# New written-out engine orders and 66 instead of 70 warming products in a fused linear-attention and MLP kernel

## The chip, the cores and the metric

The kernel runs on one NeuronCore of a Trainium2 chip. The engines named here are PE (TensorE, matrix products; PEld are its weight loads), DVE (VectorE), ACT (ScalarE), POOL (GpSimd) and SP (SyncE, which here issues every DMA). Each runs its own instructions strictly in their order; they wait for one another by semaphores. Results of products go to PSUM, which the kernel uses as eight banks of 128 partitions by 512 f32 values.

The metric is the device time of one execution in microseconds, as the median of several runs. The span of a profile goes from the first to the last instruction of one profiled execution.

## The reference

The input x is 2048 tokens by 512, in bf16. Two residual layers follow one another:

```python
# layer A: linear attention, 32 heads of 16
qkv = layernorm(x) @ wqkv                       # 512 x 1536
phi = lambda t: where(t > 0, t + 1, exp(t)) + 1e-6
pq, pk = phi(q), phi(k)
kv  = einsum("bhsd,bhse->bhde", pk, v)
z   = einsum("bhsd->bhd", pk)
o   = einsum("bhqd,bhde->bhqe", pq, kv) / (einsum("bhqd,bhd->bhq", pq, z)[..., None] + 1e-6)
h   = x + o @ wo                                # 512 x 512
# layer B: MLP with relu
out = h + relu(layernorm(h) @ w1) @ w2          # 512 x 1792, 1792 x 512
```

## The kernel before, in words

The 2048 tokens are 16 tiles of 128, in four chunks of four tiles. No scheduler sets the order. One long text, ORDER, is a list of words; the kernel goes through it from left to right and calls for each word the function `op_` of its name with the numbers behind it. So the text fixes, engine by engine, the order of the instructions. Two words on different engines have no order but what data and buffers ask for; two words on one engine run as they stand. A word can issue several instructions: `K.3.7` means the four products of the K projection of tile 3 into bank 7.

The words that matter, with their engine, and t for a tile, c for a chunk:

- Loads on SP: `lx.t.n` (n tiles of x), `lk`, `lq`, `lv`, `lo`, `l1`, `l2` (the parts k to k+n of wk, wq, wv, wo, w1, w2). SP's DMAs share eight completion semaphores in turn, so each also waits for the one eight before it.
- Warming on PE: `warm.n.b.w`, n products of zeros, w columns wide (L245).
- Layer norm of x: `S`, `A` (statistics, DVE, L248, L249), `R` (1/sqrt by a logarithm and an exponential, ACT, L254, L255), `N` (normalise, DVE, L262). Transposing a tile for the products: `T` on PE and `E` on ACT (tiles 0 to 4), or `X`, a DMA transpose issued by SP (L308, tiles 5 to 15).
- Projections on PE: `K.t` (L316, reads tile t's transposed norm as weights), `Q.c.j` (L324, reads all four tiles of a chunk).
- phi: `F` and `U` (exponential and relu out of the bank, ACT, L334, L337), `M` and `D` (DVE, L341, L344); with a `q` in front for the queries.
- State: `G.t` (PE, L368) sums the outer products over all tiles in banks 4 to 7; `gA`, `gD` take them out; `za`, `zf`, `zhi`, `zlo`, `z`, `zc`, `zh` make the sum z; `kv` (wv enters here), `kx`, `m` (wo enters here), `mA`, `mD` make the matrix that each query is multiplied with.
- Denominators: `d4` (PE), `dl4`, `dx4` (reciprocal by logarithm and exponential, ACT), `wb` (written to DRAM), `rb` (eight loads that spread each of the rows of one chunk over 16 partitions, all into one tile `rr`), `dm` (DVE: queries times reciprocal, into `pqs`, L484).
- End of layer A: `h.t` (PE, L493), `hD` (plus x, DVE, L499). Layer norm of h: `s`, `a`, `r`, `n` or `nA`; transposes by PE (`t`, `v`) for tiles 2 and 3, by SP (`x`) for the others.
- MLP: `p.c.f` (PE, L508; `ph` is half a chunk wide, L517), `pD`, `pA` (relu out of two banks, L528, L523), `f.t.b.f0.n` (PE, L537: n of the 14 products of tile t, from the f0-th on), `fo` (scaled and added to h, DVE, L545), `fd` (stored, SP, L552). Tile 15 is done in three pieces of columns.

A bank must be read by ACT or DVE before PE may write it again. The words say which bank each product uses, so the choice of banks also sets which reader PE may have to wait for. The output tiles share four buffers, tile t using t mod 4.

Of the kernel before, what the change touches and what calls it, by code (L numbers as in the profile page):

```python
# [15 lines left out]


ORDER = """
table const masks warm.70.7.64 warm.2.7 lx.0.1 S.0 A.0 R.0.1 lx.1.1 S.1 lx.2.1 A.1 N.0 T.0.1 lk.0.4 S.2 R.1.1
N.1 T.1.2 lx.3.1 A.2 E.0 K.0.4 R.2.1 lx.4.2 S.3 N.2 T.2.1 E.1 A.3 S.5 R.3.1 K.1.0.0.2 K.1.0.2.2 N.3 S.4 A.5 A.4  # L20
E.2 T.3.2 K.2.6.0.2 K.2.6.2.2 F.0.1 M.0.1 lx.6.2 E.3 S.7 lq.0.4 R.4.2 lx.8.4 Q.0.3.1 N.4 U.0.1 A.7 F.1.1 F.2.1
T.4.2 N.5 S.6 Q.0.1.4 U.1.1 M.1.1 A.6 lx.12.4 M.2.1 D.0.1 R.6.2 K.3.7.0.2 K.3.7.2.2 E.4 X.5 U.2.1 U.3.1 D.1.1
N.6 Q.0.0.3 N.7 S.10 qF.0.0.2 K.4.5 K.5.6 S.8 A.10 S.9 A.8 qU.0.0.2 S.12 F.4.2 D.2.1 X.6 Q.0.2.0 A.9 A.12 K.6.2
S.13 S.11 M.4.2 A.11 A.13 U.4.2 D.4.2 F.3.1 R.8.2 N.9 M.3.1 X.7 K.7.3 R.12.2 R.10.2 N.8 F.6.2 D.3.1 N.13 S.15
G.0 G.1 U.6.2 S.14 X.9 X.8 N.10 A.14 A.15 N.12 qM.0.0.2 M.6.2 X.13 qF.0.2.2 R.14.2 qU.0.2.2 qM.0.2.2 N.11 G.2
G.3 G.5 G.4 N.14 X.12 K.9.3 K.8.2 K.13.1 N.15 qD.0.0.2 D.6.2 za.4.1 X.11 X.10 F.8.2 U.8.2 M.8.2 K.12.0 U.12.2
F.12.2 G.7 za.6.0 K.11.3 D.8.2 qD.0.2.2 M.12.2 za.8.0 K.10.2 F.10.2 X.14 G.8 K.14.0 U.10.2 X.15 K.15.1 M.10.2 zf
lv.2.2 lv.0.2 G.9 D.10.2 zhi D.12.2 F.14.2 G.6 G.10 G.11 M.14.2 zlo U.14.2 D.14.2 z.0.0 z.2.0 z.3.0 z.1.0 G.14
lo.0.2 lo.2.2 zc zh d4.0.1 dl4.0 l1.0.2 G.13 G.12 G.15 dx4.0 gA.2.2 Q.1.1.3 Q.1.0.2 qF.1.0.2 gD.0.2 kv.1.4
kv.3.4 kv.0.4 kv.2.4 kx qU.1.0.2 qM.1.0.2 qD.1.0.2 Q.1.3.1 Q.1.2.0 qF.1.2.2 m.0.2 m.1.3 mD.0.2 m.3.7 m.2.6 wb.0  # L30
Q.2.0.4 Q.2.1.5 rb.0.7 rb.0.1 rb.0.6 rb.0.3 rb.0.0 rb.0.2 rb.0.4 rb.0.5 l1.2.2 qM.1.2.2 qU.1.2.2 Q.2.3.1
qD.1.2.2 mA.2.2 qF.2.0.2 Q.2.2.0 qU.2.0.2 dm.0.2.2 dm.0.0.2 qM.2.0.2 h.1.6 hD.1 s.1 a.1 qU.2.2.2 d4.1.3 dl4.1
h.0.7 hD.0 s.0 dx4.1 h.2.6 h.3.5 a.0 l2.0.7 wb.1 hD.2 nA.1 hD.3 qF.2.2.2 nA.0 s.2 s.3 Q.3.0.2 Q.3.1.3 a.2
Q.3.3.6 a.3 qF.3.0.2 qU.3.0.2 Q.3.2.5 x.1 r.0.4 qF.3.2.2 n.2 t.2.7 n.3 t.3.4 qD.2.0.2 v.2 v.3 x.0 ph.0.3.1.0
ph.0.1.3.0 ph.0.2.0.0 ph.0.3.1.1 qM.2.2.2 qM.3.0.2 ph.0.0.2.0 ph.0.0.2.1 qM.3.2.2 qD.3.0.2 qU.3.2.2 qD.2.2.2
ph.0.2.0.1 qD.3.2.2 p.0.7.5 d4.2.6.2 pD.0.2.2 dl4.2 dl4.3 rb.1.4 rb.1.6 rb.1.3 rb.1.2 rb.1.0 rb.1.1 ph.0.1.3.1
rb.1.7 rb.1.5 p.0.6.4 dx4.2 dm.1.0.2 dm.1.2.2 h.4.0 pD.0.0.2 hD.4 pD.0.6.2 p.0.5.1 h.6.6 dx4.3 p.0.4.0 hD.6
l2.7.7 h.5.4 pA.0.4.2 s.4 s.6 hD.5 h.7.7 a.4 a.6 p.0.11.6 p.0.10.5 s.5 hD.7 a.5 p.0.9.4 wb.2 rb.2.6 n.4 rb.2.0
rb.2.4 s.7 n.6 rb.2.3 rb.2.2 rb.2.1 a.7 n.5 n.7 rb.2.5 rb.2.7 dm.2.0.2 dm.2.2.2 pD.0.10.2 p.0.13.1 p.0.12.0
p.0.8.3 pD.0.12.2 wb.3 r.4.4 rb.3.0 rb.3.4 h.10.7 hD.10 x.6 h.8.2 h.11.6 hD.8 s.10 rb.3.5 rb.3.1 rb.3.6  # L40
f.1.0.0.7 rb.3.3 rb.3.2 rb.3.7 s.8 hD.11 pD.0.8.2 h.9.5 f.3.1.0.7 x.7 x.5 s.11 a.8 hD.9 f.1.0.7.7 f.0.4.0.7 a.10
a.11 x.4 dm.3.2.2 dm.3.0.2 h.14.7 h.12.3 s.9 n.11 h.15.6 a.9 n.10 h.13.2 fo.1 n.9 n.8 hD.14 s.14 hD.12 x.11
hD.15 f.0.4.7.7 r.8.4 p.1.13.7 p.1.6.3 a.14 hD.13 s.12 s.15 s.13 a.12 a.15 a.13 n.14 p.1.12.6 n.13 f.3.1.7.7
n.12 n.15 p.1.2.5 fo.0 pD.1.12.2 x.10 p.1.7.4 fo.3 p.1.3.6 x.9 pD.1.6.2 pD.1.2.2 r.12.4 x.8 p.1.11.2 p.1.10.1
pD.1.10.2 f.2.4.0.7 p.2.0.6 p.2.1.7 f.2.4.7.7 pD.2.0.2 p.2.10.0 p.2.11.1 fo.2 x.14 p.2.6.2 p.2.7.3 x.15 fd.3
p.2.13.7 p.2.12.6 pD.2.10.2 pD.2.6.2 x.12 fd.1 pD.2.12.2 p.2.2.0 x.13 fd.0 p.2.3.1 p.1.5.6 p.1.4.5 pD.2.2.2
pD.1.4.2 p.1.0.3 p.1.1.4 p.1.9.1 p.1.8.0 pD.1.0.2 pD.1.8.2 f.4.4.0.7 f.4.4.7.7 fo.4 fd.4 f.5.3.0.7 f.5.3.7.7
fo.5 fd.2 f.6.7.0.7 f.6.7.7.7 fo.6 p.2.4.2 p.2.5.3 f.7.0.0.7 f.7.0.7.7 pD.2.4.2 fo.7 p.3.6.1 p.3.7.2 pD.3.6.2
p.3.8.3 p.3.9.4 p.3.5.1 pD.3.8.2 p.3.4.0 pD.3.4.2 fd.6 p.3.10.3 p.3.11.4 pD.3.10.2 p.3.2.0 p.3.3.1 p.3.0.5
p.3.1.6 pD.3.2.2 pD.3.0.2 p.3.13.3 fd.7 p.3.12.2 pD.3.12.2 f.10.1.0.7 f.15.2.0.14.3.1 f.15.7.0.14.0.2 p.2.8.4  # L50
p.2.9.5 fo.15.3.1 fd.15.3.1 fo.15.0.2 pD.2.8.2 f.8.7.0.7 f.10.1.7.7 fo.10 f.8.7.7.7 fo.8 f.14.2.0.7 f.14.2.7.7
f.13.3.0.7 fd.5 fd.8 fd.10 fo.14 f.13.3.7.7 fo.13 f.9.0.0.7 f.9.0.7.7 fd.15.0.2 f.11.6.0.7 f.11.6.7.7 fd.13 fo.9
f.12.0.0.7 fd.9 f.12.0.7.7 fo.11 fd.14 fd.11 fo.12 fd.12 f.15.2.0.14.2.1 fo.15.2.1 fd.15.2.1
"""


# [1 line left out]
def kernel(  # L58
# [253 lines left out]
    def op_K(t, b, k=0, n=KD):  # L312
        c, j = divmod(t, CT)
        at_bank["k", t] = b
        for kd in range(k, k + n):
            nc.tensor.matmul(  # L316
                bk[:, b, :], lhsT=lnT[c][:, kd, j * P : (j + 1) * P], rhs=wk_sb[:, kd, :],
                start=(kd == 0), stop=(kd == KD - 1),
            )
# [213 lines left out]
    def op_f(t, b, f0, n, k=0, w=KD):  # L533
        c, j = divmod(t, CT)
        at_bank["f", t, k] = b
        for f in range(f0, f0 + n):
            nc.tensor.matmul(  # L537
                bk[:, b, 0 : w * P], lhsT=acts[c % 2][:, f, j * P : (j + 1) * P],
                rhs=w2_sb[:, f, k * P : (k + w) * P],
                start=(f == 0), stop=(f == KF - 1),  # L540
            )
# [46 lines left out]
```

## Time and profile before

| | us |
|---|---|
| median of 3 runs | 169.87 |
| lowest and highest | 169.42 to 170.21 |
| profiled span, first to last instruction | 168.0 |
| median less span | 1.87 |
| PE busy | 162.7 |
| DVE busy | 115.6 |
| ACT busy | 49.5 |

The page shows one profiled execution; it gives its span, and what lies around the span is read here as the median less the span. In its rows a number before a comma is time, `x` counts instructions, and `<-` stands between what is written and what is read. In the rows of stretches of time each engine's busy time comes with the number of its instructions in brackets; then the granted PE clock, the busy share of the DMA engines and the GB/s. In the chain of waits the columns are start, length and what the time went to. In the timeline they are start, length, engine, line, operation, and in brackets the idle time before it and what ended it; neighbouring instructions of one kind are merged, with their count. Recorded lengths of neighbouring products overlap.

### The profile page before, as it was taken

The page shows a single profiled execution, that of the slowest core. Times are in us where ns is not written, and L with a number is a line of the kernel's source. Part 1 is how long each engine was busy: PE and PEld are TensorE (multiplying, and loading weights), DVE is VectorE, ACT ScalarE, POOL GpSimd, SP SyncE. Part 2 cuts the span into 40 slices and gives each one's busy share as a digit, 9 for nine tenths or more (in the row PEclk, how much of TensorE's full clock was granted, in tenths as well). Part 3 has the DMA queues.
Part 4 walks back from the last instruction along what each step waited for, and adds up shares of the span by engine and source line. Part 5 has one row for each costly group of instructions (what it writes and reads, how often), then busy time and mean ns, then how long its engine had stood idle before and what let it go on. Part 6 is the DMA issues. An engine that isn't in the chain of part 4 may idle for free.

```text
span 168.0 us, 2417 instructions
## 1 busy us (share of the span) xinstructions
PE 162.7 (97%) x924; PEld 79.2 (47%) x924; DVE 115.6 (69%) x217; ACT 49.5 (29%) x83; POOL 4.8 (3%) x21
## 2 busy tenths in 40 slices
...
GB/s 108 353 298 88 20 106 95 189 301 45 132 337 161 98 205 132 132 48 123 83 102 57 126 63 0 0 0 0 62 31 35 0 0 7 32 34 48 31 94 39
DMA packets 25003, 16.01 MB, mean 95 GB/s; under 512 B 15008, under 2 KB 23968, under 8 KB 24992
## 3 DMA queue, kind: packets, MB, share of 16 engines
...
q8 instruction: 7, 0.11, 0.3%
q14 instruction: 4, 0.03, 0.1%
...
## 4 chain that ended last, share of the span: by engine, by line
PE 92%; DMA 4%; SPq 2%; DVE 1%; issue 0%
PE bk L537 28%; PE bk L508 27%; PE bk L324 8%; PE bk L368 8%; PE bk L493 8%; PE bk L316 7%; DMA wq_sb<-in_A_wqkv_dram 4%; PE bk L517 2%; SPq L214 2%; PE bk L440 1%; DVE gT L545 1%; PE bk L392 1%; PE bk L414 1%; PE bk L426 1%; PE bk L287 0%
## 5 line engine op out<-in xcount | busy, mean ns | idle before, releaser
L537 PE MATMUL bk<-w_sb,at 128*128 128x512 bf16 (+2 forms) x252 | 50.0, 355 | 0.0
L508 PE MATMUL bk<-lnT,w_sb 128*128 128x512 bf16 x208 | 46.9, 379 | 0.0
L528 DVE TENSOR_SCALAR at<-bk 128x1024 bf16<-128x1024 f32 x27 | 32.8, 1223 | 13.2 <-PE bk L508 13.2
L537 PEld LDWEIGHTS <-at 128*128 128x128 bf16 x252 | 23.5, 98 | 25.4
L508 PEld LDWEIGHTS <-w_sb 128*128 128x128 bf16 x208 | 20.4, 98 | 23.9
L545 DVE SCALAR_TENSOR_TENSOR gT<-bk,rstd,h_nat 128x512 bf16<-128x512 f32 (+2 forms) x18 | 12.4, 691 | 24.6 <-PE bk L537 22.0
L334 ACT ACTIVATE eb<-bk 128x1024 bf16<-128x1024 f32 (+1 forms) x18 | 16.6, 929 | 5.3 <-PE bk L316 2.8
L337 ACT ACTIVATE rb<-bk 128x1024 bf16<-128x1024 f32 (+1 forms) x18 | 16.4, 929 | 0.0
L324 PE MATMUL bk<-lnT,wq_sb 128*128 128x512 bf16 x64 | 15.1, 379 | 0.3 <-DMA wq_sb<-in_A_wqkv_dram 0.3
L316 PE MATMUL bk<-wk_sb,lnT 128*128 128x512 bf16 x64 | 15.3, 379 | 0.0
L493 PE MATMUL bk<-m_sb,pqs 128*128 128x512 bf16 x64 | 15.1, 379 | 0.0
L368 PE MATMUL bk<-at,h_nat 128*128 128x512 bf16 x56 | 13.1, 379 | 0.0
L248 DVE BATCH_NORM_STATS2 st<-x_nat 128x6 f32<-128x512 bf16 x16 | 10.6, 678 | 2.3 <-DMA x_nat<-in_A_x_dram 2.3
L499 DVE TENSOR_TENSOR h_nat<-bk,x_nat 128x512 bf16<-128x512 f32 x16 | 10.6, 676 | 0.9 <-PE bk L493 0.9
L254 ACT ACTIVATE rstd<-mv,eps 128x2 f32<-128x2 f32 (+2 forms) x14 | 4.2, 297 | 23.7 <-DVE mv L251 20.9
L250 DVE BATCH_NORM_STATS2 st<-h_nat 128x6 f32<-128x512 bf16 x16 | 10.5, 684 | 0.1
L324 PEld LDWEIGHTS <-wq_sb 128*128 128x128 bf16 x64 | 6.1, 98 | 7.7 <-DMA wq_sb<-in_A_wqkv_dram 0.8
L493 PEld LDWEIGHTS <-pqs 128*128 128x128 bf16 x64 | 6.1, 98 | 7.7 <-DVE pqs L484 0.6
L368 PEld LDWEIGHTS <-h_nat 128*128 128x128 bf16 x64 | 6.1, 98 | 7.3 <-issue 0.2
L316 PEld LDWEIGHTS <-lnT 128*128 128x128 bf16 x64 | 6.1, 98 | 6.8
L341 DVE TENSOR_SCALAR eb<-eb 128x1024 bf16<-128x1024 bf16 (+1 forms) x18 | 6.6, 389 | 0.0
L262 DVE TENSOR_SCALAR h_nat<-x_nat,mv,rstd 128x512 bf16<-128x512 bf16 x16 | 6.3, 408 | 0.2 <-ACT rstd L255 0.2
...
## 6 DMA issues: line engine op xcount, KB each, us to landing
w_sb<-in_B_w_dram SPq DMA_DIRECT2D x4, 896.0 KB, 6.2
rr<-scr SPq DMA_DIRECT2D x32, 64.0 KB, 2.6
...
x_nat<-in_A_x_dram SPq DMA_DIRECT2D x2, 256.0 KB, 4.6
...
```

The costliest lines, as they stand in the source:

```text
L248: op_S = lambda t: nc.vector.bn_stats(out=st[:, t, :], in_=x_nat[:, t, :])
L316: nc.tensor.matmul(bk[:, b, :], lhsT=lnT[c][:, kd, j * P : (j + 1) * P], rhs=wk_sb[:, kd, :], start=(kd == 0), stop=(kd == KD - 1),)
L324: nc.tensor.matmul(bk[:, b, :], lhsT=wq_sb[:, kd, j * P : (j + 1) * P], rhs=lnT[c][:, kd, :], start=(kd == 0), stop=(kd == KD - 1),)
L334: nc.scalar.activation(out=buf(eb, kind, i, n), in_=bank(at_bank[kind, i], n), func=ACT.Exp)
L337: nc.scalar.activation(out=buf(rb, kind, i, n), in_=bank(at_bank[kind, i], n), func=ACT.Relu)
L368: nc.tensor.matmul(bk[:, KD + kd, :], lhsT=ln_nat[:, t, kd * P : (kd + 1) * P], rhs=pk(t)[:, 0, :], start=(not stated), stop=(len(stated) ...
L493: nc.tensor.matmul(bk[:, b, :], lhsT=pqs[:, (c * KD + jb) % NQ, j * P : (j + 1) * P], rhs=m_sb[:, jb, :], start=(jb == 0), stop=(jb == KD ...
L499: nc.vector.tensor_tensor(out=h_nat[:, t : t + n, :], in0=bank(at_bank["h", t], n), in1=x_nat[:, t : t + n, :], op=ALU.add,)
L508: nc.tensor.matmul(bk[:, b, :], lhsT=w1_sb[:, kd, f * P : (f + 1) * P], rhs=lnT[c][:, kd, :], start=(kd == 0), stop=(kd == KD - 1),)
L528: nc.vector.tensor_scalar(out=acts[c % 2][:, f : f + n, :], in0=bank(at_bank["p", c, f], n), scalar1=-1.0, scalar2=0.0, op0=ALU.mult, op1= ...
L537: nc.tensor.matmul(bk[:, b, 0 : w * P], lhsT=acts[c % 2][:, f, j * P : (j + 1) * P], rhs=w2_sb[:, f, k * P : (k + w) * P], start=(f == 0), ...
L545: nc.vector.scalar_tensor_tensor(out=o_t[:, t % NO, cols], in0=bk[:, at_bank["f", t, k], 0 : w * P], scalar=rstd2[:, t : t + 1], in1=h_nat ...
```

## The change

The whole text ORDER is written anew. 70 small warming products become 66. The same words stand in it otherwise, apart from the bank numbers and the division of K and f into halves; so each engine does the same work in another order. Besides, the functions for K and f no longer set the first-product and last-product flags by the index of the product, but by the order in which they are called (`part`), so that the upper half of a sum may run before the lower one.

The code, and the parts of ORDER at the front, in the middle and at the end:

```diff
-table const masks warm.70.7.64 warm.2.7 lx.0.1 S.0 A.0 R.0.1 lx.1.1 S.1 lx.2.1 A.1 N.0 T.0.1 lk.0.4 S.2 R.1.1
-N.1 T.1.2 lx.3.1 A.2 E.0 K.0.4 R.2.1 lx.4.2 S.3 N.2 T.2.1 E.1 A.3 S.5 R.3.1 K.1.0.0.2 K.1.0.2.2 N.3 S.4 A.5 A.4
-E.2 T.3.2 K.2.6.0.2 K.2.6.2.2 F.0.1 M.0.1 lx.6.2 E.3 S.7 lq.0.4 R.4.2 lx.8.4 Q.0.3.1 N.4 U.0.1 A.7 F.1.1 F.2.1
-T.4.2 N.5 S.6 Q.0.1.4 U.1.1 M.1.1 A.6 lx.12.4 M.2.1 D.0.1 R.6.2 K.3.7.0.2 K.3.7.2.2 E.4 X.5 U.2.1 U.3.1 D.1.1
-N.6 Q.0.0.3 N.7 S.10 qF.0.0.2 K.4.5 K.5.6 S.8 A.10 S.9 A.8 qU.0.0.2 S.12 F.4.2 D.2.1 X.6 Q.0.2.0 A.9 A.12 K.6.2
...
+table const lx.0.1 warm.66.7.64 lx.1.1 masks lx.2.1 lk.0.4 lx.3.1 S.0 lx.4.2 S.1 lx.6.2 lq.0.4 A.1 S.2 warm.2.7
+R.1.1 lx.8.4 A.0 lx.12.4 A.2 N.1 R.2.1 T.1.2 R.0.1 N.2 E.1 N.0 T.2.0 S.3 E.2 T.0.6 K.1.1.0.2 E.0 K.1.1.2.2 A.3 S.4
+R.3.1 K.0.7 U.1.1 N.3 A.4 F.1.1 S.5 T.3.5 K.2.0.0.2 E.3 S.7 K.2.0.2.2 U.0.1 K.3.5.0.2 A.5 M.1.1 R.4.2 S.6
+K.3.5.2.2 F.0.1 Q.0.3.1 A.7 N.4 F.2.1 A.6 M.0.1 N.5 R.6.2 T.4.4 D.1.1 Q.0.0.6 X.5 U.3.1 D.0.1 N.7 E.4 Q.0.1.7 N.6
+F.3.1 S.8 X.6 U.2.1 K.4.4 M.3.1 S.9 qU.0.0.2 K.5.5 X.7 S.14 qF.0.0.2 S.12 Q.0.2.0 S.11 lv.0.2 U.4.2 K.6.2 M.2.1
...
+N.15 K.10.2 qD.0.2.2 U.12.2 za.6.0 K.11.3 X.15 F.12.2 G.7 za.8.0 F.10.2 l2.0.7 K.14.0 lo.2.2 U.10.2 lv.2.2 zf
...
+G.15 zc zh d4.0.0 G.14 dl4.0 dx4.0 G.13 wb.0 G.11 lo.0.2 Q.1.0.1 gA.2.2 gD.0.2 rb.0.6 Q.1.1.2 rb.0.7 rb.0.1 kv.1.3
+qU.1.0.2 kv.3.3 rb.0.4 kv.2.3 kv.0.3 rb.0.2 Q.1.3.7 kx qF.1.0.2 rb.0.3 rb.0.0 Q.1.2.6 qM.1.0.2 rb.0.5 m.1.1
+qD.1.0.2 l1.2.2 qF.1.2.2 m.0.0 m.3.2 l1.0.2 mD.0.2 Q.2.0.4 qU.1.2.2 Q.2.1.5 qM.1.2.2 dm.0.0.2 m.2.1 Q.2.3.6 mA.2.2
+dm.0.2.2 qD.1.2.2 h.1.7 qU.2.0.2 h.0.2 hD.1 qF.2.0.2 h.3.0 s.1 hD.0 d4.1.7 a.1 Q.2.2.5 hD.3 nA.1 s.0 h.2.0 x.1
...
-p.2.9.5 fo.15.3.1 fd.15.3.1 fo.15.0.2 pD.2.8.2 f.8.7.0.7 f.10.1.7.7 fo.10 f.8.7.7.7 fo.8 f.14.2.0.7 f.14.2.7.7
-f.13.3.0.7 fd.5 fd.8 fd.10 fo.14 f.13.3.7.7 fo.13 f.9.0.0.7 f.9.0.7.7 fd.15.0.2 f.11.6.0.7 f.11.6.7.7 fd.13 fo.9
-f.12.0.0.7 fd.9 f.12.0.7.7 fo.11 fd.14 fd.11 fo.12 fd.12 f.15.2.0.14.2.1 fo.15.2.1 fd.15.2.1
+fo.15.0.2 fo.10 fd.15.0.2 fd.4 f.14.6.0.7 f.11.2.7.7 f.11.2.0.7 f.13.0.0.7 f.13.0.7.7 f.8.1.7.7 fo.13 fd.13 fd.10
+f.8.1.0.7 fd.15.3.1 f.14.6.7.7 fo.8 fo.11 fd.8 f.12.3.7.7 fo.9 fd.11 fo.14 fd.14 f.15.0.0.14.2.1 fo.12 fd.9 fd.12
+fo.15.2.1 fd.15.2.1
...
+    fed = {}
+
+    def part(key, n):
+        at = fed[key] = fed.get(key, 0) + 1
+        return {"start": at == 1, "stop": at == n}
...
-                start=(kd == 0), stop=(kd == KD - 1),
+                **part(("k", t), KD),
...
-                start=(f == 0), stop=(f == KF - 1),
+                **part(("f", t, k), KF),
```

On SP the order of the words changes as follows; the loads up to `lx.12` and the transposes X.5 to X.7 keep their places.

```
before: X.5 X.6 X.7 X.9 ... X.15 lv.2 lv.0 lo.0 lo.2 l1.0 wb.0 rb.0(x8) l1.2 l2.0 wb.1 x.1 x.0 rb.1(x8) l2.7 wb.2
        rb.2(x8) wb.3 rb.3(x2) x.6 rb.3(x6) x.7 x.5 x.4 x.11 x.10 x.9 x.8 x.14 x.15 fd.3 x.12 fd.1 x.13 fd.0 ...
after:  X.5 X.6 X.7 lv.0 X.9 ... X.15 l2.0 lo.2 lv.2 wb.0 lo.0 rb.0(x8) l1.2 l1.0 x.1 x.0 wb.1 rb.1(x8) wb.2
        rb.2(x7) wb.3 rb.2 l2.7 rb.3(x8) x.4 x.7 x.6 x.5 x.8 x.9 x.11 fd.2 x.10 fd.6 fd.0 x.13 x.12 fd.1 x.14 fd.3 x.15 ...
```

On PE, pA's neighbourhood reads `p.0.4.4 p.0.5.5 h.7.2 ph.0.1.1.1 p.0.7.5` after the change, chunk 2's first product of h is `h.9.2`, and the first products of the third MLP chunk, `p.3.3.5 p.3.2.4`, come after `p.2.6.6`. The f products of tiles 0 to 3 and 12 to 14 are split more widely than before.

More of the change, by code (lines that the diff above doesn't have):

```diff
@@ L24 @@
[L24 to L48, printed above, removed]
@@ L49 @@
-p.3.8.3 p.3.9.4 p.3.5.1 pD.3.8.2 p.3.4.0 pD.3.4.2 fd.6 p.3.10.3 p.3.11.4 pD.3.10.2 p.3.2.0 p.3.3.1 p.3.0.5
-p.3.1.6 pD.3.2.2 pD.3.0.2 p.3.13.3 fd.7 p.3.12.2 pD.3.12.2 f.10.1.0.7 f.15.2.0.14.3.1 f.15.7.0.14.0.2 p.2.8.4
-p.2.9.5 fo.15.3.1 fd.15.3.1 fo.15.0.2 pD.2.8.2 f.8.7.0.7 f.10.1.7.7 fo.10 f.8.7.7.7 fo.8 f.14.2.0.7 f.14.2.7.7
-f.13.3.0.7 fd.5 fd.8 fd.10 fo.14 f.13.3.7.7 fo.13 f.9.0.0.7 f.9.0.7.7 fd.15.0.2 f.11.6.0.7 f.11.6.7.7 fd.13 fo.9
-f.12.0.0.7 fd.9 f.12.0.7.7 fo.11 fd.14 fd.11 fo.12 fd.12 f.15.2.0.14.2.1 fo.15.2.1 fd.15.2.1
+table const lx.0.1 warm.66.7.64 lx.1.1 masks lx.2.1 lk.0.4 lx.3.1 S.0 lx.4.2 S.1 lx.6.2 lq.0.4 A.1 S.2 warm.2.7
@@ new lines @@
+R.1.1 lx.8.4 A.0 lx.12.4 A.2 N.1 R.2.1 T.1.2 R.0.1 N.2 E.1 N.0 T.2.0 S.3 E.2 T.0.6 K.1.1.0.2 E.0 K.1.1.2.2 A.3 S.4
+R.3.1 K.0.7 U.1.1 N.3 A.4 F.1.1 S.5 T.3.5 K.2.0.0.2 E.3 S.7 K.2.0.2.2 U.0.1 K.3.5.0.2 A.5 M.1.1 R.4.2 S.6
+K.3.5.2.2 F.0.1 Q.0.3.1 A.7 N.4 F.2.1 A.6 M.0.1 N.5 R.6.2 T.4.4 D.1.1 Q.0.0.6 X.5 U.3.1 D.0.1 N.7 E.4 Q.0.1.7 N.6
+F.3.1 S.8 X.6 U.2.1 K.4.4 M.3.1 S.9 qU.0.0.2 K.5.5 X.7 S.14 qF.0.0.2 S.12 Q.0.2.0 S.11 lv.0.2 U.4.2 K.6.2 M.2.1
+D.3.1 F.4.2 A.9 S.13 K.7.3 A.8 A.11 A.13 R.8.2 A.14 qM.0.0.2 G.3 F.6.2 D.2.1 N.9 G.2 A.12 M.4.2 X.9 qF.0.2.2 N.8
```

21 lines of the change are left out of this document (added).

## The prediction

> **What bounds the kernel now.** I read the page first, then the chain of waits in order of time, then PE's busy time by stretches.
>
> ```profile
> span 168.0 us, 2417 instructions
> ...
> PE 162.7 (97%) x924; PEld 79.2 (47%) x924; DVE 115.6 (69%) x217; ACT 49.5 (29%) x83; POOL 4.8 (3%) x21
> ...
> PE 92%; DMA 4%; SPq 2%; DVE 1%; issue 0%
> ```
> ```profile
> 4.16 6.17 DMA wq_sb<-in_A_wqkv_dram
> ...
> 10.38 1.04 PE bk L324 x4
> ...
> 144.54 19.66 PE bk L537 x91
> ...
> 164.22 0.77 DVE gT L545
> ...
> 165.00 0.35 DVE gT L545
> ```
> ```profile
> 5.00:6.00 1.00, 0.49 (x5) 0.23 (x4) 1.00 (x4) 0.74 (x3) 0.81 (x4) 1.00 1.11 391
> 6.00:7.00 1.00, 0.92 (x8) 0.53 (x8) 0.49 (x3) 0.95 (x4) 0.23 (x1) 1.00 1.14 376
> ...
> 10.38:165.00 154.62, 154.59 (x824) 73.74 (x824) 108.16 (x193) 43.09 (x67) 0.00 (x0) 1.00 0.31 85
> ```
>
> PE is the bound: from 10.38 to 165.00 us it is busy 154.59 of 154.62 us. The change computes the same products, so this block cannot shrink. The time can fall only in the first 10.4 us and in the 3 us of the tail; it rises wherever the new orders open a hole in the block. The 169.87 us median is 1.87 us above the profiled span of 168.0; I take that as constant work around the span, and sum against the span.
>
> **The front.** Four warming products fewer (64 columns each) cost nothing and gain nothing: in both kernels the first transposes wait for DVE and not for them. What counts is the order on DVE, ACT and PE; these rows give the durations.
>
> ```profile
> 3.03 0.69 DVE L248 BATCH_NORM_STATS2 st<-x_nat 128x6 f32<-128x512 bf16 x1 [1.79 <-DMA x_nat<-in_A_x_dram]
> 3.76 0.18 DVE L249 BATCH_NORM_AGGREGATE mv<-st 128x2 f32<-128x6 f32 x1
> 3.86 0.66 DVE L248 BATCH_NORM_STATS2 st<-x_nat 128x6 f32<-128x512 bf16 x1
> 3.98 0.29 ACT L254 ACTIVATE rstd<-mv,eps 128x1 f32<-128x1 f32 x1 [1.90 <-DVE mv L249]
> 4.30 0.20 ACT L255 ACTIVATE rstd<-rstd 128x1 f32<-128x1 f32 x1
> 4.65 0.38 DVE L262 TENSOR_SCALAR h_nat<-x_nat,mv,rstd 128x512 bf16<-128x512 bf16 x1
> ...
> 5.09 0.40 PE L287 MATMUL bk<-ident,h_nat 128*128 128x128 bf16 x4
> ...
> 5.53 0.60 ACT L297 ACTIVATE lnT<-bk 128x512 bf16<-128x512 bf16 x1 [0.23 <-PE bk L287]
> ...
> 6.32 1.03 PE L316 MATMUL bk<-wk_sb,lnT 128*128 128x512 bf16 x4
> ...
> 6.62 0.69 DVE L248 BATCH_NORM_STATS2 st<-x_nat 128x6 f32<-128x512 bf16 x1 [0.51 <-DMA x_nat<-in_A_x_dram]
> 7.23 0.40 DVE L262 TENSOR_SCALAR h_nat<-x_nat,mv,rstd 128x512 bf16<-128x512 bf16 x1
> ...
> 14.06 1.89 PE L316 MATMUL bk<-wk_sb,lnT 128*128 128x512 bf16 x8
> ```
>
> An independent instruction follows about 0.09 us before the recorded end of the last (6.62 + 0.69 against 7.23), a dependent one 0.03 after it (3.03 + 0.69 against 3.76). Four 512-column products hold PE 0.863 us: eight in 1.73, the record of the last being longer. Four transposes hold it 0.22.
>
> Before, S, A and N of tile 0 go first. After, DVE runs S.0 3.03, S.1 3.64, A.1 4.37, S.2 4.45, A.0 5.05, A.2 5.18, N.1 5.26 to 5.67 (R.1: A.1 ends 4.54, plus 0.03, 0.29, 0.03, 0.20, so 5.1), N.2 5.97 (it waits for R.2: A.2 ends 5.35, and ACT needs the same 0.55 and 0.06 of hand-over), N.0 6.40 to 6.81. PE's first transposes so begin at 5.71 instead of 5.09, then T.2 at 6.42 and T.0 at 6.85. ACT: E.1 6.25, E.2 6.84, E.0 7.31 to 7.90. wk is there, since K.0 could start at 6.32. PE: K.1 7.07, K.0 7.94, then T.3 8.82 (S.3 6.72, A.3 7.45, R.3, N.3 8.37 to 8.78), K.2 9.04, K.3 9.90, Q.0.3 at 10.77. Before, Q.0.3 begins at 10.38, held by wq, with K.3 still to do. So: 10.38 + 0.86 - 10.77 = 0.47 us gained. The wait for wq is gone; what is late next is K.5.
>
> **The new wait: X.5.** K.5 reads tile 5 through SP's first DMA transpose, which waits for N.5.
>
> ```profile
> 11.10 16.06 SPq L308 DMA_TRANSPOSE lnT<-h_nat  x9
> ```
> ```profile
> L308 SPq DMA_TRANSPOSE lnT<-h_nat x11: 1189/1217/1831, 11.1 to 28.6; - x11
> ...
> DMA to landing us min/median/max: 2.4/2.4/3.4
> ```
> ```profile
> L214 SPq DMA_DIRECT2D x_nat<-in_A_x_dram x8: 397/431/504, 0.8 to 5.2; - x8
> ...
> DMA to landing us min/median/max: 2.0/4.0/8.7
> ```
>
> Before, X.5 goes out at 11.10, when N.5 is done, and lands 3.4 us later at 14.5, if the longest landing is the first's as the longest issue surely is; K.5 starts at 14.92, after K.4, and is not held. After, S.4, N.3, A.4, S.5, S.7, A.5, M.1, S.6, A.7, N.4, A.6 and M.0 stand before N.5, which runs 11.49 to 11.89, and X.5 goes out at 11.93. PE asks for K.5 at 10.77 + 0.86 + 0.22 + 3 x 0.863 = 14.44. With the median 2.4 X.5 lands at 14.35, hidden; with the first one's 3.4 at 15.33, 0.94 us of hole after the weight load. The nearest row is the same transfer, but its excess need not move with it: the last load of x was landing until about 13.9 (issued near 5.2, 8.7 to landing), and a delay behind that load ends at the same clock time, not 0.83 later. I take 14.6, the end that this row is nearer to, and with 0.1 for the semaphore and weight load a hole of 0.25; ends 0 and 0.94. X.6 and X.7 follow 1.3 apart and K.6 and K.7 start at 16.3 and later: covered.
>
> **SP's other moves.**
>
> ```profile
> w_sb<-in_B_w_dram SPq DMA_DIRECT2D x4, 896.0 KB, 6.2
> rr<-scr SPq DMA_DIRECT2D x32, 64.0 KB, 2.6
> ...
> wo_sb<-in_A_wo_dram SPq DMA_DIRECT2D x2, 256.0 KB, 4.9
> ```
> ```profile
> 39.43 0.34 SPq L468 DMA_DIRECT2D scr<-rd  x1
> 41.17 3.62 SPq L471 DMA_DIRECT2D rr<-scr  x8
> 44.83 0.94 SPq L220 DMA_DIRECT2D w_sb<-in_B_w_dram  x2
> ```
>
> I walk the queues on in the same way, with the rows' durations. lv.0 goes between X.7 and X.9, which waits for N.9: free. l2.0.7 passes lo.2 and lv.2: lv.2 lands by about 38, kv reads it at 42. lo.0 goes between wb.0 and the first rr load, in the 1.4 us in which SP waits for scr: free; m.0 reads wo at 45.5, landing by about 43.5, at worst (4.9) 45.4. Both l1 loads leave after rr.0, land by 54, and are read at 57.4. wb.1 goes behind x.1 and x.0, so chunk 1's rr lands about 64, with 0.8 us in hand before h.7. l2.7 leaves after wb.3, lands near 76, is read at 77.5. The second layer's transposes come just in time now: x.5 lands near 92.1 and p.1 asks at 92.6, x.15 near 124.7 and p.3 asks at 125.0. All of that is 0 if landings repeat.
>
> **Products reordered in the middle.** Whole f halves run upper half first with start and stop flags by order: no cost. m.2 moves behind Q.2.1, so mA ends only shortly before h.1 needs it.
>
> ```profile
> L429 ACT ACTIVATE m_sb<-bk 128x1024 bf16<-128x1024 f32 x1 | 1.0, 1030 | 0.0
> ...
> L523 ACT ACTIVATE at<-bk 128x1024 bf16<-128x1024 f32 x1 | 1.0, 1024 | 2.8 <-PE bk L508 2.8
> ```
>
> After m.2's last product come 0.18 (record beyond its slot) + 1.03 + 0.03 = 1.24 us; PE meanwhile has Q.2.3 (0.863) and the first two products of h.1 (0.43) = 1.29: hidden by 0.05. pA against p.0.7, which refills its bank: 1.23 against h.7 and half a ph, 1.30. Several more banks are freed with 0.05 to 0.15 us in hand. I put 0.1 on all of these, ends 0 and 0.5.
>
> **The tail.**
>
> ```profile
> 161.98 3.83 SPq L552 DMA_DIRECT2D out_dram<-gT  x3
> 164.22 1.13 DVE L545 SCALAR_TENSOR_TENSOR gT<-bk,rstd,h_nat 128x512 bf16<-128x512 f32 x2 [2.27 <-PE bk L537]
> ```
>
> The last piece is the same 128 columns of tile 15. Counted from the end of f.13: f.8 ends 3.02, f.14 4.53, f.12 6.04, f.15 6.81. DVE does fo.8, fo.11, fo.9, fo.14 back to back from 3.04 (0.66 apart) to 5.77, fo.12 6.06, fo.15 6.84 as before. But fd.14, fd.9, fd.12 and the last store now leave one behind another, 0.43 each, where fd.12 had a free queue: 0.08 later.
>
> **Sum:** 168.0 - 0.47 + 0.25 + 0.1 + 0.08 = 167.96, with 1.87 around it 169.8, my number: no measurable change. 0.5% (0.85 us) is about what a measurement of this kernel can tell from none.
>
> **Rivals.** *X.5 keeps its 3.4 us:* hole 0.94, 169.87 - 0.47 + 0.94 + 0.18 = 170.5. The first transpose's 1831 ns issue against 1217 speaks for it. *X.5 is hidden:* 169.87 - 0.47 + 0.18 = 169.6; where wq lands 1 us later than in the profile, the old order loses all of it, the new one half, and small waits may be 0: 169.0. *Slower, by rr:* after the change rr.0 leaves 0.7 us later and both dm of chunk 0 end at about 49.0, 0.2 before h.1's third product. Another us on chunk loads of rr opens 0.8 at h.1 and again some 0.5 at h.9 (dm.2 ends near 74.0, h.9 asks at 74.3): 169.8 + 1.3 = 171.1. It decides from a landing of 3.4 us instead of 2.6. Against it: nothing but wo is put in front of rr. *Slower, by the clock:* warming products start about 0.05 us apart at first and half that later:
>
> ```profile
> 3.00:4.00 1.00, 1.00 (x23) 1.00 (x21) 1.00 0.94 163
> 4.30:4.60 0.30, 0.30 (x14) 0.30 (x12) 1.00 0.94 276
> ```
>
> A us holds 21 weight loads at first, 0.3 us holds 12 later: PE has doubled its rate at about 4.3. If in the new order, where PE idles from 4.9 to 5.7 and from 5.9 to 6.4, the rise came only at about 9, T.1 to K.0 (3 x 0.22 + 2 x 0.863 = 2.4 us) would take twice as long, some 0.9 of it inside the waits for DVE: +1.5, 171.3. The page TensorE: Matmul & The Clock Gate of the Trainium skill (Part 1) says that the clock is released after a busy window of about 3.4 us that runs free of the kernel's start; by that a run may rise late in either kernel, and the new one, idler from 5 to 7, is the likelier. This trace agrees so far as the rise comes 3.2 us after the first product.
>
> **Chances.** My forecast with X.5 between 14.4 and 15: 0.45. X.5 at 3.4: 0.20. X.5 hidden and a longer wq wait gone: 0.15. rr (or a late transpose): 0.13. Clock: 0.07. Faster by over 0.5% (below 169.0): 0.12, most of the third case. Slower by over 0.5% (above 170.7): the last two, 0.20. Within: 0.68. The range from 169.0 to 170.9 leaves out the greater part of the slow cases and a few of the fast.
>
> **What would show it.** T.1, T.2, T.0 in a row before the first K, and Q.0.3 at about 10.8 without a DMA wait: the front. Idle time of PE's weight loads before the K products (L322 there, L316 here), ended by a DMA into lnT: the size of K.5's hole. Idle PE at L493 or L508: the middle. Wrong would be idle PE of over 1 us anywhere after 16 us, or slow products beyond 5 us.

## The result and the profile after

The changed kernel takes 170.66 us in the median of 8 runs (170.29 to 171.22), the kernel before 169.59 (169.14 to 170.21) on the same chip: a ratio of 1.0057 with a 95% interval of 1.0029 to 1.0085. It is slower by about 1 us, a little over the 0.5% that the prediction took for the least that can be told from no change, and the interval lies wholly above 1. The profiled execution took 170.56 us with a span of 168.8 (168.85 against 167.95 before), so the 0.90 us can be looked for in the two traces.

First the page of the changed kernel, with the chain's shares by engine, as shown of before.

```profile
span 168.8 us, 2393 instructions
...
PE 163.1 (97%) x920; PEld 79.0 (47%) x920; DVE 115.1 (68%) x217; ACT 49.5 (29%) x83; POOL 4.8 (3%) x21
...
PE 87%; DVE 6%; DMA 3%; ACT 1%; SPq 0%; issue 0%
```

PE's share of the chain fell from 92% to 87%. SPq's 2% and DMA's wait for wq have gone, and DVE has taken over the front. The next views are PE's timeline in the front (start, length, engine, line, operation) and the busy time by stretches (stretch, length, then PE, PEld, DVE, ACT, POOL).

```profile
5.74 0.40 PE L293 MATMUL bk<-ident,h_nat 128*128 128x128 bf16 x4 [0.62 <-DVE h_nat L268]
6.45 0.81 PE L293 MATMUL bk<-ident,h_nat 128*128 128x128 bf16 x8 [0.32 <-DVE h_nat L268]
...
10.85 1.03 PE L330 MATMUL bk<-lnT,wq_sb 128*128 128x512 bf16 x4
```
```profile
10.85:14.50 3.65, 3.65 (x21) 1.69 (x19) 3.65 (x13) 3.62 (x9) 0.00 (x0) 1.00 0.38 112
14.50:19.00 4.50, 3.80 (x18) 1.55 (x18) 4.50 (x17) 3.77 (x6) 0.00 (x0) 1.00 0.64 118
19.00:92.70 73.70, 73.70 (x421) 35.56 (x419) 60.22 (x115) 34.11 (x47) 0.00 (x0) 1.00 0.43 122
```

T.1 starts at 5.74, T.2 and T.0 follow from 6.45, and Q.0.3 starts at 10.85 with no wait for a DMA: the front went as walked. The block after it has one hole, 0.70 us between 14.50 and 19.00, and none from there to 92.70. The waits (engine and line, what for: us in total, times, longest) and the chain in order of time (start, length, what) name it.

```profile
PEld L322 <- DMA lnT<-h_nat: 1.6, 2, 1.2
...
PE bk L322 <- DMA lnT<-h_nat: 0.7, 1, 0.7
```
```profile
14.64 3.39 DMA lnT<-h_nat
18.07 1.04 PE bk L322 x4
```

The DMA that starts at 14.64 is X.7, the third of SP's transposes, and it lands at 18.03. K.7 starts 0.04 later. The hole costs more than the idle 0.70: the record of the last product before it runs 0.17 beyond its slot, so K.7 starts 0.87 after PE's slot was free. X.5, the transpose that the prediction was concerned with, went out at 11.99 and landed at 14.56, and K.5 was held by 0.08.

The other losses are two small waits for the second layer's transposes, and the tail is nearly unchanged. Again the chain, around chunk 3's first products and at the end.

```profile
121.95 3.45 PE bk L514 x16
125.40 0.04 issue
```
```profile
165.07 0.76 DVE gT L551
...
165.86 0.35 DVE gT L551
```

The 0.04 us before p.3.3.5 is again a wait of 0.04 + 0.17 = 0.21 by starts; it ended when x.15 landed at 125.35. The same comparison of starts gives 0.09 before p.1.1.7, behind x.5. After DVE's last operation 2.64 us remain to the end, 2.60 before. The sum of the differences is -0.40 (front, to the end of K.4) + 0.08 (K.5) + 0.87 (K.7) + 0.09 (p.1) + 0.21 (p.3) + 0.04 (tail) = 0.89, against 0.90 measured.

So the question is why X.7 took 3.39 us when the same transfer took 2.44 before. Here is the DMA view of 15.5 to 17.5 us, first of the changed kernel, then of the kernel before (queue and kind: packets, MB, share; then the transfers issued in the stretch with the time to landing).

```profile
q1 hardware_dynamic: 557, 0.14, 68.0%
q14 instruction: 1, 0.01, 2.1%
...
lnT<-h_nat SPq DMA_TRANSPOSE x1, 3.4
```
```profile
q1 hardware_dynamic: 544, 0.13, 32.8%
...
lnT<-h_nat SPq DMA_TRANSPOSE x1, 2.4
```

Two things differ: a load of wv (lv.0.2) follows X.7 on SP, whose packets are the few more on q1, and one instruction fetch of 8 KB (q14) falls into the stretch. The load is not why the share of q1 doubles: that comes mainly from longer records of X.7's own packets, up to 0.84 us each. By the trace's DMA records the fetch goes out at 15.87, together with the first of X.7's packets (15.88), and holds one of the 16 DMA engines for 0.68 us, to 16.55. Most of X.7's packets are out by 16.7, the last at 17.32, which is 1.44 us after the first; X.7 of the kernel before needs 0.76 for the same. There the fetch was at 19.64, between two transposes.

### The profile page after: what moved, and what is told of

Same layout as the page of the kernel before. It is cut to its first block, busy times and chain, and to the rows that moved or that the text cites. A ratio compares the mean times of both kernels' runs of the same rounds, so it can differ in the third digit from the quotient of the medians.

```text
span 168.8 us, 2393 instructions
## 1 busy us (share of the span) xinstructions
PE 163.1 (97%) x920; PEld 79.0 (47%) x920; DVE 115.1 (68%) x217; ACT 49.5 (29%) x83; POOL 4.8 (3%) x21
## 3 DMA queue, kind: packets, MB, share of 16 engines
q1 hardware_dynamic: 24992, 15.87, 33.0%
## 4 chain that ended last, share of the span: by engine, by line
PE 87%; DVE 6%; DMA 3%; ACT 1%; SPq 0%; issue 0%
PE bk L543 28%; PE bk L514 27%; PE bk L374 8%; PE bk L499 8%; PE bk L330 6%; PE bk L322 5%; DVE st L254 3%; PE bk L523 2%; DMA lnT<-h_nat 2%; DMA x_nat<-in_A_x_dram 1%; DVE h_nat L268 1%; PE bk L446 1%; DVE gT L551 1%; ACT lnT L303 1%; PE bk L398 1%; PE bk L420 1%
## 5 line engine op out<-in xcount | busy, mean ns | idle before, releaser
L514 PE MATMUL bk<-lnT,w_sb 128*128 128x512 bf16 x208 | 47.7, 379 | 0.0
L534 DVE TENSOR_SCALAR at<-bk 128x1024 bf16<-128x1024 f32 x27 | 32.3, 1216 | 18.8 <-PE bk L514 12.4
L330 PE MATMUL bk<-lnT,wq_sb 128*128 128x512 bf16 x64 | 15.5, 379 | 0.0
```

The lines of the kernel that those rows point to most:

```text
L330: nc.tensor.matmul(bk[:, b, :], lhsT=wq_sb[:, kd, j * P : (j + 1) * P], rhs=lnT[c][:, kd, :], start=(kd == 0), stop=(kd == KD - 1),)
L514: nc.tensor.matmul(bk[:, b, :], lhsT=w1_sb[:, kd, f * P : (f + 1) * P], rhs=lnT[c][:, kd, :], start=(kd == 0), stop=(kd == KD - 1),)
L534: nc.vector.tensor_scalar(out=acts[c % 2][:, f : f + n, :], in0=bank(at_bank["p", c, f], n), scalar1=-1.0, scalar2=0.0, op0=ALU.mult, op1= ...
```

## The experiments

The first four runs shared their runs of the kernel before (median 169.91), the next four theirs (169.74), then three (169.71) and three (169.51). Each edit is to the kernel that is named, and nothing else differs.

### The load of wv behind X.7: moved back, and moved alone

In the changed kernel lv.0.2 goes back behind X.15:

```
- ... S.11 lv.0.2 U.4.2 ...  X.15 F.12.2 ...
+ ... S.11 U.4.2 ...         X.15 lv.0.2 F.12.2 ...
```

> The changed kernel with one word moved: the load lv.0 goes back behind X.15 on SP. Theory A (an instruction fetch of 8 KB, which goes out when SP reaches its fourteenth DMA, sits on a DMA engine in front of X.7's packets): the fetch comes at X.9 again, X.7 lands 2.4 us after its issue, the 0.87 us hole before K.7 is gone, the span falls from 168.8 to about 167.9 and the time lies some 0.9 us under the changed kernel's. Theory B (the wv load itself, issued right behind X.7, takes its DMA bandwidth): the same. Theory C (X.7 is late whatever follows it, since it is issued 0.2 us later and among other work): X.7 still lands after 3.4 us and the time stays at about 170.7.

Measured: 170.45 us (170.25 to 170.93), ratio 1.0039 [1.0022, 1.0057], span 168.6. The DMA view of 15.5 to 17.5 us:

```profile
q14 instruction: 1, 0.01, 1.8%
...
lnT<-h_nat SPq DMA_TRANSPOSE x1, 3.3
```

The load has left the stretch (q1's share is still 61.0%), the fetch (15.80) has not, and X.7 is still late by 0.8, with 0.58 us of idle PE before K.7. Now the same load alone in the kernel before, and in its place a tiny one of 16 rows of 8 bytes (an added word `ty.16`):

```
- ... X.7 K.7.3 ...  zf lv.2.2 lv.0.2 G.9 ...
+ ... X.7 lv.0.2 K.7.3 ...  zf lv.2.2 G.9 ...
```

> The kernel before with the load lv.0 moved between X.7 and X.9, nothing else. Theories A and B: X.7, issued at 14.4, lands after about 3.3 us instead of 2.4, K.7 waits some 0.3 us at 17.5, span about 168.3. Theory C: X.7 lands at 16.9 as before, no hole.

```
- ... X.7 K.7.3 ...
+ ... X.7 ty.16 K.7.3 ...
```

> The kernel before with a load of 16 rows of 8 bytes (its result is not used) between X.7 and X.9. It counts as a DMA on SP's queue but moves next to nothing. Theory A: the 8 KB fetch comes at about 15.7 instead of 19.6 and X.7 lands after about 3.3 us; K.7 waits some 0.3 us. Theory B: X.7 lands after 2.4 us, no hole.

Measured, one run each: 169.33 us with a span of 167.6, and 169.80 with 168.1. X.7 takes 2.4 us in both and nothing waits for it; the fetch stays at 19.5, though in the first the big load went out right behind X.7. So neither the bandwidth of that load nor the number of transfers on SP makes X.7 late or draws the fetch. These two runs also show a thing about the front: here is PE's timeline of the first of them.

```profile
10.04 1.03 PE L323 MATMUL bk<-lnT,wq_sb 128*128 128x512 bf16 x4
```

With the old order Q.0.3 starts at 10.04 when wq lands in time, against 10.38 in the profile that the prediction was summed on. With K.3 (0.86) still to do, that is 10.90, level with the new order's 10.85.

### The second layer's transposes earlier on SP

To the kernel with lv.0.2 moved back, x.7 and x.6 go ahead of x.4, x.14 ahead of fd.6, x.15 ahead of x.13, and fd.3 behind fd.1:

```
- ... n.4 s.5 x.4 h.13.5 ...  r.4.4 x.7 h.11.4 hD.13 ...  hD.11 x.6 s.13 ...
+ ... n.4 s.5 x.7 x.6 x.4 h.13.5 ...
- ... fo.6 pD.2.12.2 fd.6 ...  pD.2.10.2 x.13 ...  fd.1 x.14 p.2.4.4 fd.3 x.15 p.2.2.0 ...
+ ... fo.6 pD.2.12.2 x.14 fd.6 ...  pD.2.10.2 x.15 x.13 ...  fd.1 fd.3 p.2.4.4 p.2.2.0 ...
```

> As the first, and on SP the second layer's transposes go ahead of stores and of each other where their data is ready: x.7 and x.6 before x.4, x.14 before fd.6, x.15 before x.13, fd.3 behind fd.1. If the 0.09 us before p.1.1 and the 0.20 before p.3.3 come from the place of x.5 and x.15 in SP's queue, both holes go and the span falls to about 167.6, against the kernel before some 0.3 us faster. If they come from DVE (n.4, n.15 late), they stay: 167.9.

Measured: 170.26 us (170.04 to 171.26), ratio 1.0024 [1.0003, 1.0045], span 168.4. The waits before p.1.1.7 and p.3.3.5 are gone, the one before K.7 is not; in the chain:

```profile
14.57 3.30 DMA lnT<-h_nat
17.92 1.04 PE bk L320 x4
```

The two small losses were the place of those transposes on SP, as the sum had it with too little in hand. What is left is X.7.

### The fetch moved by added instructions

In every trace so far, the fetch came when DVE had run the same number of instructions (waits counted): 60 or 61 in the old order, 43 in the new, whatever SP did. The counts of PE and ACT were as steady, so this alone does not name the engine. The new theory was that the fetch is for DVE's own instructions, and the next runs add idle memsets of 128x1 behind DVE's last constant. There DVE waits for x from 1.24 to 3.03 us, so they cost nothing themselves. With n = 9 in the changed kernel:

```
         nc.vector.memset(zeros[:, P:], 0.0)
+        for _ in range(9):
+            nc.vector.memset(eps5[:], 1e-5)
```

> The changed kernel with nine more memsets of one 128x1 tile on DVE behind its last constant (DVE stands idle there from 1.24 to 3.03 us; each takes 0.06 us, some 0.01 apart). Theory: the 8 KB instruction fetch that falls on X.7's packets belongs to DVE's instruction stream and goes out when DVE reaches a certain count; nine more instructions bring it forward to about 12.2 us (from 15.87), ahead of X.5's packets. X.7 then lands 2.4 to 2.6 us after its issue (3.39 in the changed kernel), the PE's idle time of 0.70 ahead of K.7 falls under 0.1, the span goes from 168.8 to 168.0-168.1, and the ratio to the kernel before to 1.000-1.002. Should the fetch meet X.5 or X.6 instead, the hole moves to K.5 or K.6 (0.3 to 0.9). Rival, that X.7 is late through the transposes and loads around it, or that the fetch belongs to another engine: fetch at 15.8-15.9, X.7 3.2-3.4 us after its issue, idle 0.6-0.7 ahead of K.7, span 168.6-168.9, ratio 1.004-1.006.

The same edit in the kernel with the second layer's transposes earlier:

> The changed kernel with its transposes x.7, x.6, x.14, x.15 earlier on SP and lv.0.2 back behind X.15 (the earlier run that took away the holes at p.1 and p.3 but not the one at K.7: span 168.4), and the nine memsets. Theory: both mendings add: no hole ahead of K.7, p.1 or p.3, span 168.42 - 0.62 = 167.8 down to 167.6, ratio to the kernel before 0.997-0.999. Rival, that X.7 is late in this order whatever is fetched: span 168.4, ratio 1.002.

Measured: 171.13 us (170.86 to 171.46), ratio 1.0077 [1.0047, 1.0108], and 170.60 (170.20 to 170.80), ratio 1.0046 [1.0029, 1.0064]. The theory was half wrong: the fetch moved, but only to 14.5 and 13.9 us, not to 12.2, and it met another transpose. The chain of the second of these kernels, and its DMA view of 13.0 to 14.6 us:

```profile
11.90 3.62 DMA lnT<-h_nat
15.57 1.04 PE bk L322 x4
```
```profile
q14 instruction: 1, 0.01, 1.2%
```

Now X.5 is the late one, with 3.6 us, and K.5 waits 0.97; X.7 is on time with 2.5. The lateness went with the fetch from X.7 to X.5, with nothing changed on SP and PE. (The first of the two lost another 0.41 in the profiled execution before T.3, by a later landing of x, which the second, with the same memsets, does not show.)

In the kernel before, n = 13:

> The kernel before with thirteen such memsets on DVE at the same place, and nothing else. Theory: the fetch moves from 19.64 to about 15.5-16.0 us, where X.7's packets run in this kernel too (issued 14.44, landed 16.88 without it); X.7 lands at 17.5-17.9, 3.1 to 3.4 us after its issue, and K.7, asked for at 17.68, starts 0.0 to 0.3 late: span 168.0 to 168.3. Rival, that the order of the changed kernel makes X.7 late: fetch at 19.5-19.7, X.7 lands 2.4-2.5 us after its issue, span 168.0.

Measured: 170.13 us (169.24 to 170.48), ratio 1.0016 [0.9993, 1.0039], span 168.4. The fetch moved from 19.64 to 14.08, not to 15.5, and fell into the gap between X.5's and X.6's packets. X.6 took 2.6 us, X.7 2.4, and PE had no hole there; the longer span is a wait of 0.43 for wq at Q.0.3. The fetch held its engine to 14.75, only 0.08 past the first of X.6's packets, and so this run could not show whether it does harm in the old order. A second try with n = 10 missed as well:

> The kernel before with ten memsets behind DVE's last constant; with thirteen its fetch went to 14.08, in the gap between X.5's and X.6's packets, and none was 0.3 late. Theory: with ten it comes a little later, 14.2 to 16.4, and falls on X.6's packets (14.3 to 15.1; X.6 then lands near 17.0 where K.6 asks at 16.8: hole 0.1 to 0.4) or on X.7's (15.6 to 16.4; X.7 lands at 17.6-17.9, K.7 asks at 17.7: hole 0 to 0.2), or in the gap between them (none late). Rival, that only the changed order makes a transpose late: all land 2.4 to 2.6 us after issue with the fetch on their packets, span 167.6-168.2.

Measured: 169.71 us (169.34 to 170.40), ratio 1.0005 [0.9987, 1.0024], span 167.7; the fetch at 13.99, in the same gap, and neither X.6 nor X.7 late behind it (DMA view of 13.6 to 14.6 us):

```profile
q14 instruction: 1, 0.01, 3.7%
```

That the old order is open to the same delay shows further on in its traces. In the kernel before and in the two single runs above, the fetch of q14 falls at 82.0, 80.9 and 81.3 us on the packets of x.4, a transpose of the second layer, and x.4 takes 3.0, 2.8 and 2.9 us. In the two runs with memsets the same fetch comes at 74.3 and 73.8 us, off x.4's packets, and x.4 takes 2.5. PE does not wait for x.4, so this costs nothing. It is a comparison of five profiles and not of runs made for it. The DMA view of the kernel before from 81.0 to 82.5 us:

```profile
q14 instruction: 1, 0.01, 1.5%
...
lnT<-hn SPq DMA_TRANSPOSE x1, 3.0
```

Three more with the new order and the second layer's transposes earlier: n = 13, n = 5, and three of DVE's own memsets moved to POOL.

> The kernel of the run with x.7, x.6, x.14 and x.15 earlier on SP (no holes at p.1 and p.3, span 168.4) with thirteen memsets behind DVE's last constant. Known so far for this order: no memset, fetch at 15.8 on X.7's packets, X.7 about 1 late; nine memsets, fetch at 13.9 on the end of X.5's packets, X.5 1.1 late and X.7 on time. Theory, that the fetch goes by DVE's count and makes late whatever transpose it meets: thirteen put it ahead of 13.0 us, where X.5's packets begin, so no transpose is late (all land 2.4 to 2.6 us after issue), no hole at K.5 or K.7, span 167.6-167.8, ratio 0.997-0.999. If it still goes out between 13.0 and 16.5, it falls on X.5, X.6 or X.7, and that one is 0.6 to 1.1 late. Rival, that one of X.5 to X.7 is late in this order whatever the fetch does: one late with the fetch off its packets, span 168.4-168.7.

> The same kernel with five memsets behind DVE's last constant. Theory: the fetch lies between the two places known, 15.8 (none) and 13.9 (nine), so on X.6's packets (14.5 to 15.3) or in one of the gaps ahead of them or behind (14.2 to 14.5, 15.3 to 15.7). On X.6's: X.6 lands 3.2 to 3.5 us after issue, at 16.5 to 16.8 where K.6 asks for it at 16.2, so a hole of 0.3 to 0.6 ahead of K.6, and X.7 on time; span 168.0-168.4. In a gap: no transpose late, span 167.6-167.8, ratio 0.997-0.999. Rival, that X.7 is late in this order: X.7 3.3 us after issue wherever the fetch is, span 168.4.

```
-        nc.vector.memset(eps5[:], 1e-5)
-        nc.vector.memset(eps6[:], 1e-6)
-        nc.vector.memset(ones[:], 1.0)
+        nc.gpsimd.memset(eps5[:], 1e-5)
+        nc.gpsimd.memset(eps6[:], 1e-6)
+        nc.gpsimd.memset(ones[:], 1.0)
```

> The same kernel with three of DVE's five memsets (the two epsilons and the ones) moved to POOL, and no memset added: DVE has three instructions fewer ahead of its first statistics. Theory: DVE reaches the fetch three instructions later in its work, at 16.4 to 17.0 us in place of 15.8, behind most of X.7's packets (15.7 to 16.5); X.7 lands 2.4 to 2.7 us after issue if the fetch is behind 16.5, 3.0 to 3.4 if it still meets them; span 167.6-167.9 in the first case, 168.2-168.5 in the second. The ident mask stands 0.2 to 0.3 later on POOL, hidden ahead of T.1 at 5.7. Rival, the fetch not bound to DVE: it stays at 15.8 and X.7 lands 3.3 after issue, span 168.4.

Measured:

| edit to the new order, small transposes mended | fetch at, us | on the packets of | late transpose, us to landing | hole | span | time, us | ratio to before |
|---|---|---|---|---|---|---|---|
| none | 15.8 | X.7 | X.7, 3.3 | K.7, 0.62 | 168.4 | 170.26 | 1.0024 [1.0003, 1.0045] |
| 5 memsets | 15.7 | X.6 (its end) | X.6, 3.5 | K.6, 0.47 | 168.7 | 170.02 | 1.0019 [1.0000, 1.0039] |
| 9 memsets | 13.9 | X.5 (its end) | X.5, 3.6 | K.5, 0.97 | 168.7 | 170.60 | 1.0046 [1.0029, 1.0064] |
| 13 memsets | 12.5 | none | none, at most 2.6 | none | 167.7 | 169.57 | 0.9990 [0.9970, 1.0011] |
| 3 memsets to POOL | 22.3 | none | none, at most 2.6 | none | 167.5 | 169.74 | 0.9990 [0.9969, 1.0010] |

With five, the profiled execution started late (x landed later, 0.28 lost before T.3) and X.6 with it, so that the fetch at 15.7 met X.6's last packets. The rows of the two without a hole: with thirteen, the DMA view of 12.3 to 13.3 us and the landing times of all eleven transposes; with three on POOL, the DMA view of 21.9 to 23.0.

```profile
q14 instruction: 1, 0.01, 3.3%
```
```profile
L314 SPq DMA_TRANSPOSE lnT<-h_nat x11: 1189/1216/1287, 12.0 to 28.4; - x11
...
DMA to landing us min/median/max: 2.4/2.5/2.6
```
```profile
q14 instruction: 1, 0.01, 2.5%
```

Whichever of X.5, X.6 and X.7 had the fetch on its packets came about 1 us late, and no other did. Without it the new order is level with the kernel before, and not measurably faster.

### POOL alone, and the changed kernel with nothing else mended

Three memsets on POOL had both left DVE and joined POOL. So three small ones were added on POOL alone, in the kernel with the second layer's transposes earlier:

```
+        for _ in range(3):
+            nc.gpsimd.memset(mask[:, 0:1], 1.0)
         make_identity(nc, ident[:])
```

> The kernel with x.7, x.6, x.14 and x.15 earlier on SP, with three small memsets added on POOL ahead of its first mask and nothing changed on DVE. Theory, that the fetch is DVE's: it stays at 15.7-15.9 on X.7's packets, X.7 lands 3.2-3.4 us after issue, idle of 0.6-0.7 ahead of K.7, span 168.3-168.6. Rival, that POOL's instructions or the layout of all code set it (POOL got three more where DVE got three fewer): the fetch moves by over 1 us, as far as 22, and X.7 lands 2.5 us after issue with no hole, span 167.5-167.8.

Measured, one run: 170.26 us, span 168.6. The DMA view of 15.5 to 17.5 us has the fetch (15.81) and the late X.7 as without the edit, and PE idles 0.51 before K.7:

```profile
q14 instruction: 1, 0.01, 2.2%
...
lnT<-h_nat SPq DMA_TRANSPOSE x1, 3.2
```

POOL's instructions do not move it. Last, the three memsets of DVE moved to POOL in the changed kernel itself, with the loads and transposes as the change has them:

> The changed kernel itself, with three of DVE's memsets moved to POOL and no other edit (its loads and transposes stand as in the change). Theory: the fetch leaves X.7's packets (to about 22 us as in the mended kernel), X.7 lands 2.5 us after issue, no hole ahead of K.7, while the small holes ahead of p.1 and p.3 (0.09 and 0.20) stay: span 168.85 - 0.70 = 168.1, 167.8 to 168.2, ratio to the kernel before 1.000-1.003. Rival, that the early lv.0.2 holds X.7 too: X.7 still 0.4 to 0.9 late with the fetch away, span 168.4-168.8, ratio 1.004-1.006.

Measured: 169.98 us (169.67 to 170.32), ratio 1.0026 [1.0012, 1.0039], span 168.1. The stretch that lost 0.70 is full, no first-layer transpose is late, and the wait before p.3 is still there (busy time by stretch; landing times; chain):

```profile
14.50:19.00 4.50, 4.50 (x23) 1.93 (x22) 4.50 (x17) 4.47 (x7) 0.00 (x0) 1.00 0.48 117
```
```profile
DMA to landing us min/median/max: 2.4/2.5/2.6
```
```profile
121.22 3.45 PE bk L514 x16
124.68 0.04 issue
```

So the fetch alone carries the hole before K.7, and the early lv.0.2 adds nothing to it. The ratio goes from 1.0057 over 1.0026 to 0.9990. By these medians the fetch costs about 0.3% (the first two intervals overlap; by the spans, 168.8 to 168.1, it is 0.4%), and the two small waits (0.17 and 0.21 us by starts in this execution) are most of the rest.

### The 66 warming products

In the changed kernel `warm.66.7.64` becomes `warm.70.7.64`.

> The changed kernel with 70 small warming products in place of 66, the only edit of its own. Theory: worth nothing; T.1 starts at 5.7 us as before, the hole ahead of K.7 stays (X.7 3.2 to 3.5 us after its issue), span 168.7-168.9. Rival, that the four products moved the clock's rise or the first transposes: T.1 or the rise by over 0.1 us elsewhere, and the span with it.

Measured, one run: 170.34 us, span 168.6, X.7 3.4 us to landing, idle 0.73 before K.7. T.1 starts at 5.54, 0.2 earlier than in the profile of the changed kernel. The kernels with 66 have it between 5.52 and 5.79, so the earlier start is the landing of x, and one run tells no more of the four products than that they are worth less than 0.2 us. One thing did move: the first fetch of the other instruction queue (q8, 16 KB) goes out at 10.45 us here and between 11.15 and 11.69 in the other fifteen traces.

## Why the prediction was wrong

The forecast was 169.8 us, from 169.0 to 170.9, and no measurable change. The measured 170.66 lies in the range, but the kernel is measurably slower. The number is close to the 170.5 of the rival "X.5 keeps its 3.4 us", and that is chance: X.7 was late, not X.5.

**The front: right on its execution, wrong as a gain.** The walk held within 0.1 us: T.1 5.74 for 5.71, Q.0.3 10.85 for 10.77, no wait for wq, 0.40 gained for 0.47. But it was summed against one execution, in which Q.0.3 waited 0.33 us for wq. Of four more profiles of the old order, two show such a wait and two do not, and those two reach the same point at 10.86 and 10.90. So most of the 0.47 was the bad luck of one profile, and the new order without its holes is level with the old one (0.9990).

**The new wait, X.5: right, with some luck.** It went out at 11.99 for 11.93, landed at 14.56 for 14.6, and cost 0.08 for 0.25. The 14.6 was a point between 14.35 and 15.33, chosen from the one row with 3.4; X.5 took 2.57, and 2.56 or 2.57 in every profile of the new order in which no fetch met its packets.

**"X.6 and X.7 follow 1.3 apart and K.6 and K.7 start at 16.3 and later: covered": this is the step that failed.** They did follow 1.3 us apart, but X.7 took 3.39 us instead of the 2.4 that the step took for it, and the 0.87 it cost is nearly the whole difference of the spans, 0.90. The cause is an instruction fetch that the new order moved onto its packets, from 19.64 to 15.87. The prediction had a row with a longest landing of 3.4 and gave it to X.5, as a delay behind the last load of x that need not move with it; to X.6 and X.7 it gave the median without asking what else could be late. In that execution a fetch too (16 KB, queue q8, 11.43 to 12.51) stood ahead of X.5's packets: x's last three packets go out after it, from 12.50 to 13.29, and X.5's last 34 from 13.46 on. In the five profiles of the old order that fetch ends 0.9, 1.2, 1.2, 1.4 and 1.4 us after X.5's issue, and X.5 takes 2.6, 2.9, 2.9, 3.2 and 3.4. So the fetch is the likely cause there too, though no run set out to move it.

**SP's other moves: "0 if landings repeat" was too thin.** x.15 was put 0.3 ahead of its reader and cost 0.21; x.5 was put 0.5 ahead and cost 0.09. The order run shows that their place on SP was all of it.

**Products reordered in the middle: right**, 0 for 0.1, with PE busy 73.70 of 73.70 us. **The tail: right**, 0.04 for 0.08. **The rivals:** X.5 did not keep its 3.4, rr opened nothing, and the products ran at full speed from the first K on, so the clock rival is out in this execution. A late transpose stood in the chances only as a parenthesis of the rr rival, with no place and no price. By the prediction's own mark, idle PE after 16 us would show it wrong; the 0.70 us at 17.4 is that, somewhat under the 1 us it named.

What stays open is the rule by which the fetch is placed. It belongs to DVE's instructions: it moved in seven of the eight runs that changed their number (in the eighth, with five added, it stayed at 15.7 us while the work around it ran 0.4 later), and in none that changed SP, PE or POOL alone; the number of ACT's instructions was never changed. But it did not move one for one: 22.3 to 22.5 us with three fewer, 15.7 to 15.9 with none or five added, 13.9 to 14.5 with nine, 12.5 with thirteen. Nor did it where the old order got ten and thirteen (13.99 and 14.08 from 19.6). Its place could not have been worked out from the kernel before. That it stood somewhere among the transposes, and could meet one, could.
